# Masking by a minimum on the exponentials, turning left values through DRAM, and an order list for each group

## The chip, the cores and the metric

The kernel runs on one core of one Trainium2 chip. The metric is the device time of one execution, in microseconds; three executions of the kernel before gave 852.54, 853.44 and 858.74, median 853.44.

## The reference, cut to what matters

Two attention layers share one input `x` of 2048 rows by 512 and are mixed row by row with a gate: `g * a + (1 - g) * b`.

```python
# A: 64 segments of 32 rows, 32 heads of 128, 8 memory rows carried along
for s in range(n_seg):
    h = concatenate([mem, x[s]])                  # 8 + 32 rows
    q, k, v = h @ Wq, h @ Wk, h @ Wv              # per head
    scores = where(mask, q @ k.T * scale, -1e9)   # mask: idx_q < 8 or idx_q >= idx_k
    o = (softmax(scores) @ v) @ Wo
    mem = o[:8]; outs.append(o[8:])
# B: 4 blocks of 512 rows, 32 heads of 16, causal softmax attention in the block,
#    plus a linear-attention memory (M, z) of the blocks before, mixed by sigmoid(beta)
```

Segment `s + 1` of A needs the memory rows that segment `s` puts out; B does not depend on A.

## The kernel before, in words

**A.** A group is four consecutive segments. Only 32 of a segment's 40 rows are computed in the chain: 8 memory rows and the first 24 rows of `x`. The last 8 rows of each of the four segments ("left" rows) are projected together, 32 rows at once, ahead of time for the next group (`left_units`): units KL0, KL1, QL0, QL1, VL0, VL1, each a projection of 16 heads on TensorE (L1031 with xL), an evacuation (L387 or L389) and a transpose of 32x32 blocks on VectorE (`flip` L1043, `flip_rows` L1048). Left values are then turned back by matmuls against the identity (units vt0 and vt1, L1090) and evacuated to VL, so that the values of one segment's left rows lie together.

A segment (`segment(s)`) does everything for two halves b of 16 heads, in units that an order list names as `r.unit`, r being the segment in its group:

- `Q0x Q0y K0x ... V1y`: half projections, each two of four 128-row chunks (L1031 with hT); `q0 k0 v0 ...`: evacuations; `TK0 TQ0 ...`: transposes on VectorE; `qt`: GpSimd copies the left queries in.
- `S0 S1`: scores into one PSUM bank, keys as rows. First four matmuls add the mask, `mneg`, by multiplying it with the identity (L1279), then 16 per-head products for the 40 queries (L1282), then 8 products for the left keys (L1287).
- `X0 X1`: exponential on ScalarE into P_sb (L1296). `M0 M1`: sums over keys by matmuls with blocks of ones (L1313). `L0 L1`: logarithm and exponential of the negative on ScalarE, giving 1/sum (L1320, L1323). `N0 N1` on VectorE (L1327) and `n0 n1` on GpSimd (L1333): normalisation.
- `PV0 PV1` and `PL0 PL1`: products with the values (L1343) and the left values (L1355); `E0a ... E1b`: evacuations; `W0a ... W1b`: products with Wo (L1111); `H0 H1`: evacuations; `F0 F1`: folds of four partial sums (L1129); `hm0 hm1`: memory rows into the next segment's hT; `ax0 ax1`: the other rows; `oL`, `xc`: GpSimd copies.
- `ol0 ol1 of`: the output product of a group's left rows, done a group later.

**B** is cut into units that fill A's waits: `bS` (scores, L835), `bE` (exponential of 1024 columns, L854, then a triangle cut on GpSimd), `bP` (values, L887), `bT` (closing work, which has 24 products with the memory, L927). B's own projections come before A, from 5 to 62 us. `tl tb tf` load and write the mixed output of 128 rows.

**Order.** Each engine runs its queue in order. A Python planner walks an order list and appends each unit's operations to the queues of its engines; waits follow from what is read and written. A unit with `e` at the end is the second part of a unit begun before. Units of B and the tail that are not due are skipped, and `relief` runs one when PSUM banks run out. There are three lists: `A_FIRST` for groups 0 to 2, `A_GROUP` for 3 to 14, `A_LAST` for 15. Left units of group 0 run ahead of the lists, one after another:

```python
for u in ("KL0", "KL1", "QL0", "QL1", "VL0", "VL1", "vt0", "vt1"):
    run(first, u)
    run(first, u + "e")
```

DMAs to and from DRAM are issued on SP's queue, in order, each after its waits; A's weights Wk, Wq and Wv are loaded from ScalarE's queue.

Of the kernel before, what the change touches and what calls it, by code (L numbers as in the profile page):

```python
# [5 lines left out]
ALU = mybir.AluOpType  # L6
# [251 lines left out]
def build(nc, es, A_x, A_mem0, A_Wq, A_Wk, A_Wv, A_Wo, B_wq, B_wk, B_wv, B_wo, B_beta, gate_w, out, dbg=None):  # L258
# [31 lines left out]
    def alloc(stack, *specs):  # L290
        at, spans = 0, {}
        for name, shape, dt, n in specs:
# [15 lines left out]
          ("onesb", [128, 128], BF16, 0), ("mneg", [128, 224], BF16, 0),  # L308
# [4 lines left out]
          ("aTg", [128, C, 128], BF16, 0), ("fold", [128, SEG], F32, 0), ("VTL", [128, 4, H // 2, 8, 2], BF16, 0),  # L313
# [3 lines left out]
          ("bmask", [128, 136], BF16, 0), ("mskT", [128, 2, 2, 8, 2], BF16, 0), ("mem0_sb", [128, DM], BF16, 0), ("gwr_sb", [128, 128], BF16, 0), ("beta_sb", [128, HB], BF16, 0),  # L317
# [6 lines left out]
    RT = [128, 4, H // 2, 8, 2]  # L324
    in_a = alloc(esA, ("xL", [128, C, SEG], BF16, 0), ("LN_sb", [128, 2, 512], BF16, 0), ("KTL0", RT, BF16, 0), ("QTL0", LT, BF16, 0), ("VL0", [128, 2, 512], BF16, 0),
          ("KN_sb", [128, 2, 512], BF16, 0), ("QN_sb", [128, 2, 512], BF16, 0), ("KT_sb", LT, BF16, 0), ("QT_sb", [128, H // 2, L, 2], BF16, 0),
          ("V_sb", [128, 2, 512], BF16, 0), ("P_sb", [128, 2, 224], BF16, 0), ("R_sb", [128, 2, 160], F32, 0),
          ("OT_sb", [128, H, L], BF16, 0), ("OTL", [128, H, SEG], BF16, 2), ("KTL1", RT, BF16, 0), ("QTL1", LT, BF16, 0), ("VL1", [128, 2, 512], BF16, 0),
# [13 lines left out]
    dram("aTd", [NG, 128, C, 128])  # L342

# [96 lines left out]
def plan_const(v):  # L440
# [3 lines left out]
    ident, onesb, mneg = v.ident, v.onesb, v.mneg  # L444
    NEG = -1.0e9
# [24 lines left out]
    def late():  # L470
        rob, rmk = Rs("onesb"), Rs("mneg")
        gp(lambda g: g.memset(onesb[:], 0.0), rob, "onesb0", True)
        gp(lambda g: g.memset(mneg[:], 0.0), rmk, "mneg0", True)
        rmt = Rs("mskT")
        gp(lambda g: g.memset(v.mskT[:], NEG), rmt, "mskT0", True)
        for n in range(2):
            gp(lambda g, n=n: g.memset(v.mskT[:, n, n, :, :], 0.0), rmt, "mskT0")
# [4 lines left out]
        for j in range(4):  # L482
            q = slice(32 * j, 32 * j + 32)
            gp(lambda g, q=q: g.memset(onesb[q, q], 1.0), rob, "onesb1_%d" % j)
            for i in range(4):
                o = (L + 16) * i
                sel(mneg[q, o + M:o + L], [[1, 32]], ALU.is_ge, NEG, M, -1, rmk, "mneg1_%d" % j)
            for n in range(2):
                row = v.mskT[q, n, n, :, :]
                for u in range(2):  # L490
                    sel(row[:, :, u], [[-1, 8]], ALU.is_ge, NEG, -16 * u - 8, 1, rmt, "mskT1_%d" % j)
                    sel(row[:, :, u], [[0, 8]], ALU.is_ge, 0.0, -16 * u - 8, 1, rmt, "mskT2_%d" % j)
                    sel(row[:, :, u], [[0, 8]], ALU.is_ge, NEG, -16 if u else 15, 1 if u else -1, rmt, "mskT3_%d" % j)
        v.late_mask = lambda: P.op("dve", lambda d: d.transpose(mneg[:, :].rearrange("p (i w) -> p i w", w=L + 16)[:, :, L:L + 16], v.mskT[:, :, :, :, :].rearrange("p n m k u -> p (n m) (k u)")),
# [276 lines left out]
class BAttn:  # L771
# [178 lines left out]
A_FIRST = """  # L950
    bP bP bT bS 0.Q0x tl bE tl bE 0.Q0y 0.K0x 0.K0y 0.Q1x tb tf 0.q0 bE bT 0.qt 0.Q1y 0.K1x 0.k0 0.K1y 0.TK0 0.q1 bP 0.TQ0 bP 0.TQ1 0.k1 bS 0.V0x 0.S0
    bP bP 0.TK1 0.V0y 0.S1 0.V1x 0.X0 0.V1y 0.M0 QL1 0.X1 0.M1 bE bT 0.v1 0.L0 tbe 0.n0 0.v0 0.N0 tbe VL0 0.xc tf 0.L1 0.PV0 bT tfe 0.PL0 0.n1 KL1 bP
    0.N1 0.E0b 0.E0a 0.PV1 0.PL1 0.W0b 0.E1a 0.E1b 0.W0a 0.W1a tf 0.W1b bP VL1 bT 0.H0 0.F0 tf 0.H1 0.F1 bT tfe 0.hm0 0.hm1 QL0 tl 0.ax0 0.ax1 tf bS
    1.Q0x 1.Q0y 1.K0x 1.Q1x 1.q0 1.K0y bE 1.K1x bE 1.K1y 1.Q1y 1.qt bP 1.k0 1.TQ0 tf 0.oL 1.k1 bE bP 1.TK0 bS tl 1.TK1 bP 1.S0 1.q1 tf 1.V0x 1.TQ1 bS
    1.V1x 1.S1 bP 1.X0 tb 1.M0 bE 1.V0y 1.X1 tfe 1.M1 bT tb tb 1.L0 tfe bE 1.v0 1.V1y tf 1.N0 1.L1 bP tbe bE 1.n0 1.PV0 1.xc bE 1.n1 1.PL0 QL1e 1.E0b
    1.N1 KL0 1.v1 1.E0a 1.PV1 1.PL1 1.W0b 1.E1a 1.E1b 1.W0a bT 1.W1a tbe 1.W1b 1.H0 bS tb bT tfe 1.F0 1.H1 tl 1.oL tl 1.hm0 1.F1 1.hm1 bP 2.qt 2.Q0x
    1.ax0 2.K0x 2.Q0y tbe bT bE bT bS 1.ax1 bE 2.K0y 2.k0 2.Q1x VL1e tfe 2.Q1y bT 2.K1x 2.K1y 2.q0 2.q1 2.TQ0 2.TK0 2.S0 VL0e 2.k1 tl bP tb bP tfe
    2.TQ1 KL1e bS 2.TK1 2.V0x tb 2.X0 bS tl KL0e 2.M0 2.S1 2.V0y 2.V1x ol0 2.L0 2.X1 bP 2.M1 tbe tf 2.n0 2.V1y 2.v0 2.N0 bE 2.PV0 2.PL0 tl 2.L1 2.E0a
    2.v1 2.E0b ol1 bP 2.n1 tb 2.N1 tb 2.PV1 tfe 2.PL1 ol1e 2.W0a 2.E1a 2.E1b 2.W0b 2.W1a 2.W1b vt0 2.H0 bE bS tb tb bT tbe 2.F0 2.H1 2.hm0 2.F1 3.qt
    2.hm1 bP 2.xc 3.K0x vt0e 2.ax0 3.Q0x bP tf bP 3.K0y 3.Q0y bP tfe 3.Q1x 3.K1x 3.Q1y 2.ax1 3.q0 bS 3.k0 bP 3.K1y 3.V0x 3.q1 tl 2.oL 3.TQ0 3.TK0 3.k1  # L960
    tf 3.S0 3.X0 3.TQ1 3.TK1 bE 3.V0y 3.V1x 3.S1 3.M0 3.X1 3.V1y 3.L0 3.v0 tfe of bE 3.M1 3.v1 3.L1 3.n0 3.N0 3.PV0 3.N1 3.n1 3.PL0 3.E0a bE 3.xc bE
    3.PV1 3.PL1 3.W0a 3.E1b QL0e 3.E0b 3.E1a 3.W0b 3.W1b 3.W1a vt1 bS bE bE 3.H0 3.F0 3.H1 tl 3.F1 vt1e bP tbe 3.hm0 3.ax0 3.hm1 bS bT 3.oL tf tf ofe
    3.ax1
    """.split()
A_GROUP = """
# [35 lines left out]
def plan_a(v, nseg):  # L1001
# [48 lines left out]
    def four(t, r, m):  # L1050
        return t[:, r, m, :, :].rearrange("p m k u -> p (m k u)")
# [507 lines left out]
```

## Time and profile before

| | |
|---|---|
| median of three runs | 853.44 us |
| profiled execution | 852.41 us, span 850.6 |
| TensorE matmul | 824.1 us busy (97%), 23047 instructions |
| TensorE weight load | 451.0 (53%) |
| VectorE | 573.9 (67%), 1219 instructions |
| ScalarE | 578.7 (68%), 1412 |
| GpSimd | 252.4 (30%), 619 |
| granted TensorE clock | 1.00 |
| DMA | 51.29 MB, mostly in the first 80 us |

Busy time is the union of an engine's instructions. In a row of a group of instructions, the numbers after the bar are the busy time in us, the mean duration of one in ns, and the idle time of the engine just before them with what ended it. In a timeline row they are start, duration, engine, line, operation, output<-inputs, shape, count.

### The profile page before, as it was taken

To read this page: it belongs to the slowest core of one execution; us is meant where nothing else is said; L and a number is where in the kernel's file an instruction comes from. 1 tells how busy PE (TensorE), PEld (TensorE's weight loads), DVE (VectorE), ACT (ScalarE), POOL (GpSimd) and SP (SyncE) were. 2 spreads that over 40 slices of the span, in tenths; PEclk is the share of its full clock that TensorE was granted. 3 is DMA by queue.
4 is the path that set the end of the run, shared out by engine and by line. 5 is a ranking of instruction groups with operands and counts; after the bars stand their busy time and mean duration, and the time that the engine had idled before them with its cause. 6 is when DMAs were issued, how large, how long until landed. Compare 5 with 4: busy or idle time off the path is not lost.

```text
span 850.6 us, 50542 instructions
## 1 busy us (share of the span) xinstructions
PE 824.1 (97%) x23047; PEld 451.0 (53%) x23054; DVE 573.9 (67%) x1219; ACT 578.7 (68%) x1412; POOL 252.4 (30%) x619
## 2 busy tenths in 40 slices
PE   8998999999999999999999999999999999999997
PEld 4644454555555555555556555555555555555554
DVE  4856566665776767676776767677676767677654
ACT  5765876777677676767676676766767676767554
POOL 3611332323232322333232323233233233223210
PEclk9999999999999999999999999999999999999999
DMA  9997110000011010111111011111111011110011
GB/s 326 407 400 251 22 42 22 16 24 23 23 34 26 20 39 20 33 33 33 30 25 34 21 28 29 33 32 34 30 23 37 20 26 34 32 42 5 16 47 40
DMA packets 63581, 51.29 MB, mean 60 GB/s; under 512 B 33920, under 2 KB 59784, under 8 KB 61832
## 3 DMA queue, kind: packets, MB, share of 16 engines
q1 hardware_dynamic: 61640, 35.48, 14.7%
q10 hardware_dynamic: 1728, 12.58, 3.6%
q8 instruction: 181, 2.97, 1.5%
q14 instruction: 32, 0.26, 0.1%
HBM read 33.47 MB, written 14.57 MB: 56 GB/s over the span
## 4 chain that ended last, share of the span: by engine, by line
PE 89%; DVE 4%; ACT 3%; DMA 2%; issue 1%; DVEq 0%; ACTq 0%
PE ps L1031 48%; PE ps L1111 17%; PE ps L1129 4%; PE ps L1343 3%; PE ps L676 2%; DVE V_sb L389 2%; PE ps L835 2%; PE ps L887 2%; PE ps L1199 1%; PE ps L1282 1%; PE ps L1279 1%; PE ps L1313 1%; DMA scr_kqd<-stgk 1%; DVE P_sb L1327 1%; PE ps L700 1%; DMA Wv_sb<-in_A_Wv_dram 1%
## 5 line engine op out<-in xcount | busy, mean ns | idle before, releaser
L861 POOL TENSOR_SCALAR_AFFINE_SELECT PT<-PT 128x256 bf16<-128x256 bf16 (+2 forms) x160 | 88.5, 553 | 269.8 <-ACT PT L854 264.6
L854 ACT ACTIVATE PT<-ps 128x1024 bf16<-128x1024 f32 x160 | 161.6, 1026 | 5.7 <-PE ps L835 5.5
L1031 PE MATMUL ps<-Wq_sb,hT 128*32 128x512 bf16 x2048 | 144.4, 380 | 0.4 <-ACT hT L387 0.3
L1031 PE MATMUL ps<-Wv_sb,hT 128*32 128x512 bf16 x2048 | 140.7, 379 | 0.7 <-issue 0.4
L1031 PE MATMUL ps<-Wk_sb,hT 128*32 128x512 bf16 x2048 | 139.6, 379 | 0.1
L1111 PE MATMUL ps<-Wo_sb,OT_sb 128*32 128x512 bf16 x2048 | 124.3, 380 | 0.0
L387 ACT ACTIVATE OT_sb<-ps 128x320 bf16<-128x320 f32 x192 | 76.6, 434 | 47.3 <-PE ps L1355 47.0
L389 DVE CAST V_sb<-ps 128x512 bf16<-128x512 f32 x128 | 87.2, 684 | 22.4 <-PE ps L1031 21.8
L387 ACT ACTIVATE KN_sb<-ps 128x512 bf16<-128x512 f32 x128 | 77.1, 602 | 32.9 <-PE ps L1031 31.1
L1333 POOL TENSOR_TENSOR P_sb<-P_sb,R_sb 128x64 bf16<-128x64 bf16 x128 | 48.9, 382 | 145.6 <-ACT R_sb L1323 142.6
L1043 DVE STREAM_TRANSPOSE KT_sb<-KN_sb 128x256 f32<-128x256 f32 x128 | 55.9, 437 | 53.6 <-ACT KN_sb L387 53.3
L387 ACT ACTIVATE WF<-ps 128x256 f32<-128x256 f32 x128 | 42.2, 381 | 73.1 <-PE ps L1111 73.1
L1031 PEld LDWEIGHTS ps<-Wk_sb,hT 128*32 128x32 bf16 x2048 | 55.2, 97 | 49.8 <-ACT PT L854 2.4
L1031 PEld LDWEIGHTS ps<-Wq_sb,hT 128*32 128x32 bf16 x2048 | 53.8, 96 | 50.2 <-ACT hT L387 3.0
L389 DVE CAST QN_sb<-ps 128x512 bf16<-128x512 f32 x64 | 43.8, 684 | 53.5 <-PE ps L1031 53.5
L1043 DVE STREAM_TRANSPOSE QT_sb<-QN_sb 128x256 f32<-128x256 f32 x128 | 56.9, 444 | 25.5 <-ACT QN_sb L387 21.7
L1111 PEld LDWEIGHTS ps<-Wo_sb,OT_sb 128*32 128x32 bf16 x2048 | 48.6, 96 | 44.9 <-ACT OT_sb L387 2.5
L1296 ACT ACTIVATE P_sb<-ps 128x224 bf16<-128x224 f32 x128 | 45.7, 357 | 25.0 <-PE ps L1313 12.6
L389 DVE CAST LN_sb<-ps 128x512 bf16<-128x512 f32 x80 | 54.3, 679 | 10.5 <-PE ps L1031 9.0
L1031 PEld LDWEIGHTS ps<-Wv_sb,hT 128*32 128x32 bf16 x2048 | 46.2, 95 | 26.6 <-ACT KN_sb L387 2.2
L389 DVE CAST OT_sb<-ps 128x320 bf16<-128x320 f32 x64 | 31.3, 489 | 33.1 <-PE ps L1355 33.1
L1320 ACT ACTIVATE R_sb<-ps 128x160 f32<-128x160 f32 x128 | 38.4, 300 | 16.9 <-PE ps L1313 16.1
(132 smaller groups left out, 1433.0 us busy)
## 6 DMA issues: line engine op xcount, KB each, us to landing
Wk_sb<-in_A_Wk_dram ACTq DMA_DIRECT2D x4, 1024.0 KB, 7.8
scr_kqd<-stgk SPq DMA_DIRECT2D x16, 256.0 KB, 7.7
Wq_sb<-in_A_Wq_dram ACTq DMA_DIRECT2D x4, 1024.0 KB, 7.7
Wv_sb<-in_A_Wv_dram ACTq DMA_DIRECT2D x4, 1024.0 KB, 7.7
Wo_sb<-in_A_Wo_dram SPq DMA_DIRECT2D x8, 512.0 KB, 6.8
scr_vd<-V SPq DMA_DIRECT2D x16, 136.0 KB, 6.7
Vj<-scr_vd SPq DMA_DIRECT2D x32, 68.0 KB, 2.5
Wo_sb<-in_A_x_dram SPq DMA_DIRECT2D x8, 256.0 KB, 6.5
```

What stands on the lines that cost most here:

```text
L387: P.op("act", lambda a: a.activation(dst, src, ACT.Copy), reads=[v.rbank[k] for k in bks], writes=dres, name=name)
L389: P.op("dve", lambda d: d.tensor_copy(dst, src), reads=[v.rbank[k] for k in bks], writes=dres, name=name)
L854: P.op("act", lambda a: a.activation(pt[:, :, :], v.ps[:, bks[0]:bks[1] + 1, :], ACT.Exp, scale=v.SCALE_B), reads=[v.rbank[b] for b in bks ...
L861: P.op("gp", lambda g: g.affine_select(mv, mv, [[0, 2], [0, len(cut)], [1, 128]], ALU.is_ge, 0.0, base=0, channel_multiplier=-1), reads=[r ...
L1031: ins = pe.matmul(pb[bk][SEG * j:SEG * (j + 1), :], lhs(c), cols(w, j) if split else w[:, 512 * j:512 * (j + 1)], start=(c == 0), stop=(c ...
L1043: P.op("dve", lambda d: d.transpose(to, src), reads=reads, writes=writes, name=name)
L1111: ins = pe.matmul(pb[bk][SEG * j:SEG * (j + 1), :], lhs(4 * k + j), Wo_sb[:, 4 * k + j, :], start=(first and k == ks[0]), stop=False, skip ...
L1129: ins = pe.matmul(pb[bk][SEG * j:SEG * (j + 1), SEG * n:SEG * (n + 1)], part[:, o:o + SEG], v.fold[:, :], start=True, stop=True, skip_grou ...
L1296: P.op("act", lambda a: a.activation(P_sb[:, b, :], pb[bk][:, 0:224], ACT.Exp, scale=SCALE), reads=[rbank[bk]], writes=[Rs("P%d" % b), Rs( ...
L1320: P.op("act", lambda a: a.activation(R_sb[:, b, :], pb[bk][:, 224:384], ACT.Ln), reads=[rbank[bk]], writes=[Rs("R%d" % b)], name="ln%d_%d" ...
L1333: P.op(ENG["n"], lambda d: d.tensor_tensor(left(P_sb), left(P_sb), grp04(R_sb[:, b, :]), ALU.mult), reads=[Rs("R%d" % b)], writes=[Rs("P%d ...
L1343: ins = pe.matmul(pb[bks[j]][:, L * i:L * (i + 1)], V_sb[SEG * j:SEG * (j + 1), b, i * E:(i + 1) * E], P_sb[SEG * j:SEG * (j + 1), b, LW * ...
```

## The change

The scores are no longer masked in PSUM: the four matmuls per half go, and a new unit `Y0`/`Y1` takes, on VectorE, the minimum of P_sb and `mkeep` (0 where masked, 3e38 elsewhere) between the exponential and the sums. Left rows are ordered row first and segment second. The left values are evacuated as they come into VNL, stored to DRAM when both halves are there, and loaded back by four DMAs into VL, in place of the transposes and of vt0 and vt1; the transposes of the left keys become two each. Each group has a list of its own, which also holds the copy `xl` and, in group 0, that group's own left units (`i` in front). The lists of groups 0 to 14 hold 80 bS, 160 bE and 160 bP among them, the list of group 15 none. The last segment's rows are also marked as written to the tail's input. All lists but part of one are left out here.

```diff
-          ... ("onesb", [128, 128], BF16, 0), ("mneg", [128, 224], BF16, 0),
+          ... ("onesb", [128, 128], BF16, 0), ("mkeep", [128, 224], BF16, 0),
-          ("aTg", [128, C, 128], BF16, 0), ("fold", [128, SEG], F32, 0), ("VTL", [128, 4, H // 2, 8, 2], BF16, 0),
+          ("aTg", [128, C, 128], BF16, 0), ("fold", [128, SEG], F32, 0), ("VNL", [128, 2, 512], BF16, 0),
+    dram("vld", [NG, 128, 2, 4, 128])
-    NEG = -1.0e9
+    KEEP = 3.0e38
-        gp(lambda g: g.memset(mneg[:], 0.0), rmk, "mneg0", True)
+        gp(lambda g: g.memset(mkeep[:], KEEP), rmk, "mkeep0", True)
-                sel(mneg[q, o + M:o + L], [[1, 32]], ALU.is_ge, NEG, M, -1, rmk, "mneg1_%d" % j)
+                sel(mkeep[q, o + M:o + L], [[1, 32]], ALU.is_ge, 0.0, M, -1, rmk, "mkeep1_%d" % j)
...
+A_LIST7 = """
+    0.Q0x 0.Q1x bE 0.Q0y xl 0.K0x 0.qt 0.Q1y 0.q0 0.K0y bE 0.TQ0 0.k0 0.TK0 0.K1x 0.K1y 0.q1 0.V0x 0.xc 0.V0y 0.TQ1 0.k1 0.TK1 0.S0 0.X0 0.V1x 0.S1 tf
+    0.V1y 0.v0 0.Y0 0.M0 0.X1 0.L0 0.n0 bP 0.Y1 tfe bP 0.M1 0.L1 0.N0 0.n1 KL0 0.N1 1.qt 0.PV0 0.PL0 0.E0a 0.E0b 0.v1 KL1 0.PV1 tl 0.PL1 0.E1a 0.W0b 0.E1b
...
     def flip_rows(dst, nat, reads, writes, name):
-        to = dst.rearrange("p r m k u -> p m r (k u)").bitcast(F32)
-        src = nat.bitcast(F32).rearrange("p (m a e) -> p m a e", a=4, e=8)
-        P.op("dve", lambda d: d.transpose(to, src), reads=reads, writes=writes, name=name)
-
-    def four(t, r, m):
-        return t[:, r, m, :, :].rearrange("p m k u -> p (m k u)")
+        src = nat.bitcast(F32).rearrange("p (j m k r) -> p m j k r", m=2, k=8, r=4)
+        for m in range(2):
+            to = dst[:, :, :, :, m, :].bitcast(F32)[:, :, :, :, 0].rearrange("p r j k -> p j k r")
+            P.op("dve", lambda d, to=to, m=m: d.transpose(to, src[:, m, :, :, :]), reads=reads, writes=writes, name=name)
...
-        P.op("gp", lambda gq: gq.tensor_copy(
-            xL[:, :, :].rearrange("p c (r i) -> p c r i", i=8),
-            xT[:, :, 128 * g:128 * (g + 1)].rearrange("p c (r t) -> p c r t", t=SEG)[:, :, :, SEG - 8:SEG]),
-             reads=x_all, writes=[Rs("xL")], name="xl%d" % g)
-        units = {}
+
+        def x_left():
+            P.op("gp", lambda gq: gq.tensor_copy(
+                xL[:, :, :].rearrange("p c (i r) -> p c i r", r=4),
+                xT[:, :, 128 * g:128 * (g + 1)].rearrange("p c (r t) -> p c t r", t=SEG)[:, :, SEG - 8:SEG, :]),
+                 reads=x_all, writes=[Rs("xL")], name="xl%d" % g)
+
+        values = []
+
+        def turn_values():
+            P.dma(P.group("vs%d" % g, "vs"), lambda s: s.dma_start(v.vld[g].rearrange("p b a e -> p b (a e)"), v.VNL[:, :, :]),
+                  reads=[Rs("VNL0"), Rs("VNL1")], writes=[Rs("vld%d" % g)], name="stl%d" % g)
+            grp = P.group("vl%d" % g, "vl")
+            rows = v.vld[g].rearrange("(q r) b a e -> a q (r b) e", r=4)
+            for a in range(4):
+                P.dma(grp, lambda s, a=a: s.dma_start(VL[par][a:128:4, :, :], rows[a]),
+                      reads=[Rs("vld%d" % g)], writes=[Rs("VL%d_%d" % (par, b)) for b in range(2)], name="ldl%d_%d" % (g, a), scratch=True)
+        units = {"xl": x_left}
...
-                    proj(bk, lhs, w_sb, b, True, [Rs("xL"), Rs(wr)], "%sL%d_%d" % (m, g, b))
+                    proj(bk, lhs, w_sb, b, m != "V", [Rs("xL"), Rs(wr)], "%sL%d_%d" % (m, g, b))
                     return lambda: u2(bk, m, b)
 
                 def u2(bk, m, b):
+                    if m == "V":
+                        evac(ENG["VL%d" % b], v.VNL[:, b, :], pb[bk], [bk], [Rs("VNL%d" % b)], "VLev%d_%d" % (g, b))
+                        B.give(bk)
+                        values.append(b)
+                        if len(values) == 2:
+                            turn_values()
+                        return
...
-                    dst, res = (v.VTL, "VTL%d" % b) if m == "V" else (KTL[par] if m == "K" else QTL[par], "%sTL%d_%d" % (m, par, b))
+                    dst, res = KTL[par] if m == "K" else QTL[par], "%sTL%d_%d" % (m, par, b)
...
-                        flip_rows(dst[:, :, 8 * b:8 * (b + 1), :, :], LN_sb[:, b, :], [Rs("LN%d" % b)], [Rs(res)], "%sLt%d_%d" % (m, g, b))
+                        flip_rows(dst[:, :, 4 * b:4 * (b + 1), :, :, :], LN_sb[:, b, :], [Rs("LN%d" % b)], [Rs(res)], "%sLt%d_%d" % (m, g, b))
                 units["%sL%d" % (m, b)] = u
-        for b in range(2):
-            def t(b=b):
...
             def f_sc(pe):
                 ins = None
-                for j in range(4):
-                    rows = slice(SEG * j, SEG * (j + 1))
-                    pe.matmul(pb[bk][rows, 0:224], ident[:, rows], mneg[:, :], start=True, stop=False, skip_group_check=True)
                 for i in range(4):
                     for j in range(4):
                         ins = pe.matmul(pb[bk][SEG * j:SEG * (j + 1), LW * i:LW * i + L], head(KT_sb, 16 * b + 4 * j + i),
-                                        head(QT_sb, 16 * b + 4 * j + i), start=False, stop=True, skip_group_check=True)
+                                        head(QT_sb, 16 * b + 4 * j + i), start=True, stop=True, skip_group_check=True)
                 for k in range(2):
                     for j in range(4):
                         m = 8 * b + 2 * j
-                        ins = pe.matmul(heads4(pb[bk][SEG * j:SEG * (j + 1), 0:4 * LW])[:, 2 * k:2 * k + 2, L:LW], four(KTL[par], r, slice(m, m + 2)),
+                        ins = pe.matmul(heads4(pb[bk][SEG * j:SEG * (j + 1), 0:4 * LW])[:, 2 * k:2 * k + 2, L:LW], KTL[par][:, r, m // 2, :, :, :].rearrange("p k m u -> p (k m u)"),
                                         QT_sb[:, m + k, :, :].rearrange("p (a q) u -> p u a q", q=8)[:, :, 0::4, :],
-                                        start=False, stop=True, skip_group_check=True)
+                                        start=True, stop=True, skip_group_check=True)
                 return ins
-            P.op("pe", f_sc, reads=[Rs("KT%d" % b), Rs("QT%d" % b), Rs("QTl"), Rs("KTL%d_%d" % (par, b)), Rs("mneg"), Rs("ident")],
+            P.op("pe", f_sc, reads=[Rs("KT%d" % b), Rs("QT%d" % b), Rs("QTl"), Rs("KTL%d_%d" % (par, b))],
                  writes=[rbank[bk]], name="sc%d_%d" % (s, b))
 
         def expo(b):
             bk = sbk[b]
             P.op("act", lambda a: a.activation(P_sb[:, b, :], pb[bk][:, 0:224], ACT.Exp, scale=SCALE),
                  reads=[rbank[bk]], writes=[Rs("P%d" % b), Rs("P%dL" % b)], name="exp%d_%d" % (s, b))
+
+        def mask(b):
+            P.op(ENG["y"], lambda d: d.tensor_tensor(P_sb[:, b, :], P_sb[:, b, :], mkeep[:, :], ALU.min),
+                 reads=[Rs("mkeep")], writes=[Rs("P%d" % b), Rs("P%dL" % b)], name="msk%d_%d" % (s, b))
...
-                    ins = pe.matmul(grp04(pb[bks[j]][:, 0:4 * L]), VL[par][SEG * j:SEG * (j + 1), b, 128 * r:128 * (r + 1)],
+                    ins = pe.matmul(grp04(pb[bks[j]][:, 0:4 * L]), VL[par][SEG * j:SEG * (j + 1), 2 * r + b, :],
...
-            P.op("gp", lambda gq: gq.tensor_copy(QT_sb[:, :, SEG:L, :], QTL[par][:, :, 8 * r:8 * r + 8, :]),
+            P.op("gp", lambda gq: gq.tensor_copy(QT_sb[:, :, SEG:L, :], QTL[par][:, :, r:SEG:4, :]),
...
-    for u in ("KL0", "KL1", "QL0", "QL1", "VL0", "VL1", "vt0", "vt1"):
-        run(first, u)
-        run(first, u + "e")
-    rest = {}
+    rest = {"i" + u: fn for u, fn in first.items()}
...
-        for u in ORDERS[2 if ending else g > 2]:
+        for u in ORDERS[g]:
```

## The prediction

> **What bounds the kernel now.** I read the page's busy times first, then the groups of instructions by shape, then TensorE's timeline for one segment, then the chain in order of time.
>
> ```profile
> span 850.6 us, 50542 instructions
> PE 824.1 (97%) x23047; PEld 451.0 (53%) x23054; DVE 573.9 (67%) x1219; ACT 578.7 (68%) x1412; POOL 252.4 (30%) x619
> PEclk9999999999999999999999999999999999999999
> ```
>
> TensorE looks full at a full clock, VectorE and ScalarE are two thirds full. The timeline shows what TensorE's 97% is made of (start, duration, instruction):
>
> ```profile
> 405.37 0.60 PE L1031 MATMUL ps<-Wv_sb,hT 128*32 128x512 bf16 x8
> 405.81 0.27 PE L1279 MATMUL ps<-mneg,ident 128*32 128x224 bf16 x4
> 405.90 0.27 PE L1282 MATMUL ps<-QT_sb,KT_sb 128*32 128x40 bf16 x16
> 406.00 0.21 PE L1287 MATMUL ps<-QT_sb,KTL 128*32 128x32 bf16 x8
> 406.06 1.03 PE L1031 MATMUL ps<-Wv_sb,hT 128*32 128x512 bf16 x16
> 406.92 0.27 PE L1313 MATMUL ps<-P_sb,onesb 128*32 128x160 bf16 x8
> 409.00 0.41 PE L1090 MATMUL ps<-ident,VTL 128*32 128x128 bf16 x16
> 409.24 1.03 PE L1199 MATMUL ps<-woB_sb,oTg 128*32 128x512 bf16 x16
> ```
>
> A matmul's duration includes a pipeline that the next one overlaps, so what an item costs is the distance from its start to the next start: a half projection 0.43, the four mask products 0.09 to 0.10, the scores without them 0.155, the sums 0.095, a turn of left values (L1090) 0.22 to 0.24. Read so for every unit from the first left projection (about 60.8) to 847, the items make 722 us of 786: 64 us are waits, most of them hidden inside "busy". The chain shows the rhythm, one group of four segments being the distance between two equal rows:
>
> ```profile
> 305.88 4.00 PE ps L1031 x72
> 353.83 4.00 PE ps L1031 x72
> 401.98 4.00 PE ps L1031 x72
> ```
>
> That is 48.1 us a group, with items for 45.2: waits 2.9. The first three groups take about 50.6 with items for 44.8: waits 5.8. So TensorE's own work bounds the kernel, and the chain from one segment's memory to the next one's is close behind it.
>
> **The parts of the change, costed.** These rows carry the prices:
>
> ```profile
> L1279 PE MATMUL ps<-mneg,ident 128*32 128x224 bf16 x512 | 35.0, 260 | 0.0
> L1090 PE MATMUL ps<-ident,VTL 128*32 128x128 bf16 x512 | 12.8, 220 | 1.1 <-DVE VTL L1048 1.1
> L1327 DVE TENSOR_TENSOR P_sb<-P_sb,R_sb 128x160 bf16<-128x160 bf16 x128 | 42.2, 331 | 5.8 <-ACT R_sb L1323 5.5
> L664 DVE TENSOR_SCALAR etmp<-etmp 128x512 bf16<-128x512 bf16 x24 | 7.1, 294 | 2.2 <-ACT etmp L659 2.1
> L389 DVE CAST VL<-ps 128x512 bf16<-128x512 f32 x32 | 21.9, 688 | 6.1 <-PE ps L1090 5.9
> L1048 DVE STREAM_TRANSPOSE VTL<-LN_sb 128x256 f32<-128x256 f32 x32 | 14.2, 445 | 1.1
> ```
>
> *TensorE.* The mask products go: 128 half segments by 0.095 = 12.2 us. The turns go: 32 by 0.22 = 7.0 us. Together **-19.2 us**. Both stand behind their waits, in the order of the queue, so they are not hidden by anything. The Trainium skill ("Perfetto Trace Analysis", Identifying the Most-Contended Engine) says that matmul busy time misjudges pipelined work; the trace agrees, since the busy column would promise 35.0 + 12.8 = 47.8 us for the same two groups, and with that the kernel would come to about 808.
>
> *VectorE.* Added: 128 minima of 128x224. Nothing in the trace is a two-source bf16 operation throughout. Low end: L664 does 512 elements of one source in 294 ns, so 0.22 to 0.29. High end: L1327 scaled, 331 + 64 elements at 0.96 a ns = 0.40. I take 0.33, between, as L1327 is the nearest by operation but has an f32 source. The Trainium skill ("VectorE: DVE Perf Modes", the perf-mode tier table) has a bf16 tensor_tensor at two elements a cycle, which I estimate at 0.27; no row here shows it. Gone: 32 casts by 688 = 21.9 and 32 transposes by 445 = 14.2. The 32 KTL transposes become 64 of half the size; from 445 less 128 elements at one per 1.04 ns, 0.31 each, +5.7. Net 42 - 36 + 6 = +12 us over 790, from 67% to about 70%: not a bound by itself.
>
> *The wait.* The minimum comes between the exponential and the sums. The smallest distance that the trace has from the start of the mask products to the sums is 0.93, so 0.68 from the end of the scores; now 0.68 plus the minimum plus a hand-over of about 0.05, or 1.0 to 1.13. Behind the waiting minimum in VectorE's queue stand V casts, transposes and normalisations; behind the waiting sums stand the next projections. What covers it is what the list puts between S and M: before, 0.90 in the median; in the new lists 1.19, with 0.96 for a quarter of the halves. The cover was lengthened by about the price. If it were not there, 128 by 0.35 = 45 us would show.
>
> *The lists.* The three old lists name B units that are often not due; the new ones name exactly the 80 score, 160 exponential and 160 value units that there are, all in the first fifteen groups, as now (the last B product in the profile is at 785.9). So no item is added or lost by them.
>
> *Left values through DRAM.* Per group one store of 256 KB and four loads of 64 KB on SP's queue, 80 issues in all. Nearest rows: 256 KB landed in 7.7 us while the weights loaded, 64 KB (pQj) in 2.5, and one issue took 0.3 to 0.6. The loads wait for the store, so SP is held for 4 to 8 us a group, and behind it stand the K, Q and V loads of B, the tail's loads and the output stores. SP idles most of the span, and from VL1's evacuation to the next group's PL0 the lists leave some 24 us: nothing, after group 0. In group 0 the store stands behind the Wo loads, issued until 72.7, with the DMA engines busy until about 79; then four issues and 2.5 us land the values at about 84. PL0 is due 14.7 us of items after 60.8, near 79 with waits: **+5 us**.
>
> *The start.* The first left units now stand between projections. Now they take 8.7 us (60.8 to 69.5) for 5.6 of items: **-3 us**; the late Wv (a wait of 1.4) is covered by two half projections and B scores.
>
> *GpSimd* keeps its copies, the mask constants their number: 0.
>
> **The sum.** -19.2 + 5 - 3 = -17, if the waits stay what they are: 2.9 a group in the steady part. The profiled execution took 852.4 (span 850.6 and 1.8 around it), 1.0 under the median of the runs; so 835.4 in its terms, 836.4 against the median, rounded to **837**.
>
> **The rivals.**
> *The chain takes over (within 1%).* I went down both orders of TensorE with the smallest distances that the trace shows (S to M above; sums to PV 1.5; V pass to PV 1.0; last Wo product to the two folds 0.65 and 0.95; fold to the next projection 0.5), adding each shortfall once. Before: 1.6 of the 2.9 us in a steady group, 35 in all. After: 2.8 a steady group, 57 in all, of which some 2 go for the 24 B memory products that I left out. That is +20 and gives 837 + 20 = 857, or about 850 if lists made per group lose less behind busy ScalarE and VectorE than the remaining 29 us of today. For it: less TensorE work is left to fill the same chain. Against: the smallest distances are not the ones that an order sees, and the first three groups show that waits follow the list (5.8 against 2.9 with almost equal items).
> *Slower: the minimum stands behind casts.* In VectorE's order by the new lists, 38 of 128 minima come right after a V or left-value cast of 0.68 and 50 after a transpose of 0.44. If each is late by half of that, 38 by 0.34 + 50 by 0.22 = 24 us, on top of the +20 with half of it overlapping: 837 + 32 = 869. It decides once the sums start more than some 1.2 us after the scores end, the median cover. For it: VectorE is in order and 70% full. Against: the cast is placed there because the exponential is still running.
> *Better lists.* If the waits fall by a third everywhere, 64 to 43: 837 - 21 = 816. For it: 29 us are waits that no dependence explains. Against: less work to fill with.
> *No saving at all* would need mask products that ran in a wait; the timeline has them behind their wait, without a gap.
>
> **How the numbers follow.** Forecast (waits stay) 0.42, better lists 0.10, chain takes over 0.30, minimum behind casts 0.18. The measurement tells about 1% (8.5 us) from no change. Faster by more than that: the first two less a little of the forecast's edge, plus the chain's lower edge: 0.52. Same: 0.27. Slower: 0.21. The range reaches from the better lists' near half, 818, to 864, between the two slower cases; the likeliest case alone, with the minimum at 0.22 or 0.40 and the group 0 wait at 0 or 8, has 828 to 845.
>
> **What would show it.** Right: no mask and turn products, some 22,000 matmul records; 47.0 us a steady group with items for 44.0; minima near 0.3; PL0 of group 0 waiting about 5 us for a DMA and no DMA wait later; VectorE near 70%. Wrong: a steady group at 48 with waits before the sums or PV (chain), minima whose releaser is a cast (second rival), B's K, Q or V loads late behind the left values' loads, or a clock under full after group 0's wait.

## The result, and the profile after

The kernel after takes 860.34 us (median of 12 runs, 857.55 to 865.50) against 853.36 for the kernel before on the same chip: a ratio of 1.0075, with a 95% interval of 1.0049 to 1.0100. The prediction had 837 and faster; it came out slower by three quarters of a per cent, inside the range of 818 to 864 but on the other side of no change.

The page of the kernel after, first the span and busy times, then the granted clock in 40 slices:

```profile
span 859.2 us, 48664 instructions
PE 816.6 (95%) x22030; PEld 425.3 (49%) x22030; DVE 572.9 (67%) x1315; ACT 582.7 (68%) x1412; POOL 255.7 (30%) x619
PEclk9999899999999999999999999999999999999999
```

TensorE is less busy, by 1,017 matmuls, in a longer span, and one slice is under the full clock. The added operation costs what it should; groups by shape on VectorE, with busy time and mean ns after the bar:

```profile
L1453 DVE TENSOR_TENSOR P_sb<-P_sb,mkeep 128x224 bf16<-128x224 bf16 x128 | 36.2, 285 | 11.3 <-ACT P_sb L1449 9.6
L1205 DVE STREAM_TRANSPOSE KTL<-LN_sb 128x128 f32<-128x128 f32 x64 | 26.2, 409 | 2.2
L390 DVE CAST VNL<-ps 128x512 bf16<-128x512 f32 x32 | 21.9, 687 | 14.4 <-PE ps L1187 8.5 <-DMA scr_vld<-VNL 5.7
```

The third row holds a first clue: VectorE stood 5.7 us before a cast, for the store of the left values.

I measured groups from the first sums of one to the first sums of the next, in TensorE's timeline. Counted by their columns, at the rate of the half projections (0.43 us for 2 x 512), TensorE's items from the first sums to the last product shrank from 687.4 to 667.2 us, by 20.2 where 19.2 was forecast; what lies between them grew from 82.8 to 110.4.

| us | first sums at | group 0 | 1 | 2 | mean of 3 to 13 | 14 | 15, to the end |
|---|---|---|---|---|---|---|---|
| before | 76.8 | 50.0 | 51.1 | 49.2 | 48.15 | 47.1 | 46.8 |
| after | 78.1 | 60.1 | 49.8 | 48.2 | 48.23 | 46.2 | 46.4 |

So there are two losses: 10 us in group 0, and a steady group in which 1.2 us less work takes as long as before. Group 0 first, all engines' timeline (SPq is a DMA issue):

```profile
75.98 1.26 SPq L1222 DMA_DIRECT2D scr_vld<-VNL  x1
78.39 1.13 PE L1187 MATMUL ps<-Wq_sb,xL 128*32 128x512 bf16 x16
83.33 2.50 SPq L1227 DMA_DIRECT2D VL<-scr_vld  x4
83.33 0.69 DVE L390 CAST VNL<-ps 128x512 bf16<-128x512 f32 x1 [5.66 <-DMA scr_vld<-VNL]
84.54 0.55 DVE L1484 TENSOR_TENSOR P_sb<-P_sb,R_sb 128x160 bf16<-128x160 bf16 x2
85.00 0.32 PE L1500 MATMUL ps<-P_sb,V_sb 32*128 32x40 bf16 x16 [5.48 <-DVE P_sb L1484]
88.72 0.24 PE L1512 MATMUL ps<-P_sb,VL 32*128 32x64 bf16 x4 [3.40 <-DMA VL<-scr_vld]
88.89 1.90 PE L1187 MATMUL ps<-Wq_sb,xL 128*32 128x512 bf16 x16
```

The store is issued at 75.98, behind the Wo loads, and has landed at 83.33. VL0e of the *next* group writes the same VNL, so its cast waits for that store, and the normalisations stand behind the cast in VectorE's queue: TensorE waits 5.48. Only then do the four loads come, and TensorE waits another 3.40. The last row is a projection at half speed (1.90). Before, the same products followed one another without a wait, and a left projection took 1.05:

```profile
79.02 0.27 PE L1343 MATMUL ps<-P_sb,V_sb 32*128 32x40 bf16 x16
79.13 0.20 PE L1355 MATMUL ps<-P_sb,VL 32*128 32x64 bf16 x4
79.26 1.05 PE L1031 MATMUL ps<-Wk_sb,xL 128*32 128x512 bf16 x16
```

The stretch after by windows: TensorE's busy time, then the granted clock, the DMA share and GB/s:

```profile
80.00:82.00 2.00, 0.00 (x0) 1.00 0.56 204
82.00:84.00 2.00, 0.00 (x0) 0.70 0.05 20
90.00:92.00 2.00, 2.00 (x40) 0.50 0.00 0
92.00:94.00 2.00, 2.00 (x36) 0.74 0.04 8
```

For the steady groups the timeline shows one place well: segment 1, from the products with left values (PL0) to the next half's products with values (PV1). Before:

```profile
433.11 0.20 PE L1355 MATMUL ps<-P_sb,VL 32*128 32x64 bf16 x4
433.23 0.30 PE L887 MATMUL ps<-PT,Vj 128*32 128x128 bf16 x8
433.36 0.40 PE L1090 MATMUL ps<-ident,VTL 128*32 128x128 bf16 x16
433.96 0.28 PE L1343 MATMUL ps<-P_sb,V_sb 32*128 32x40 bf16 x16 [0.21 <-DVE V_sb L389]
```

And after:

```profile
441.62 0.21 PE L1512 MATMUL ps<-P_sb,VL 32*128 32x64 bf16 x4
441.76 0.30 PE L888 MATMUL ps<-PT,Vj 128*32 128x128 bf16 x8
442.47 0.28 PE L1500 MATMUL ps<-P_sb,V_sb 32*128 32x40 bf16 x16 [0.41 <-ACT OT_sb L388]
```

0.85 us with a turn of left values in it, 0.85 without: that turn seems to have run in a wait, which an experiment below tests.

### The profile page after: what moved, and what is told of

Read it like the earlier page. It is cut to its first block, busy times and chain, and to the rows that moved or that the text cites. A ratio compares the mean times of both kernels' runs of the same rounds, so it can differ in the third digit from the quotient of the medians.

```text
span 859.2 us, 48664 instructions
## 1 busy us (share of the span) xinstructions
PE 816.6 (95%) x22030; PEld 425.3 (49%) x22030; DVE 572.9 (67%) x1315; ACT 582.7 (68%) x1412; POOL 255.7 (30%) x619
## 4 chain that ended last, share of the span: by engine, by line
PE 86%; ACT 5%; DMA 4%; DVE 3%; issue 1%; POOL 0%; SPq 0%; DVEq 0%; POOLq 0%; ACTq 0%
PE ps L1187 45%; PE ps L1266 17%; PE ps L1284 4%; PE ps L1500 3%; PE ps L677 3%; PE ps L836 3%; PE ps L888 2%; PE ps L1470 2%; PE ps L1355 2%; PE ps L1435 2%; PE ps L701 1%; DVE V_sb L390 1%; DMA Wv_sb<-in_A_Wv_dram 1%; DMA scr_kqd<-stgk 1%; ACT PT L855 1%
## 5 line engine op out<-in xcount | busy, mean ns | idle before, releaser
L855 ACT ACTIVATE PT<-ps 128x1024 bf16<-128x1024 f32 x160 | 159.4, 1026 | 1.3 <-PE ps L836 0.6
L1187 PE MATMUL ps<-Wq_sb,hT 128*32 128x512 bf16 x2048 | 136.2, 380 | 0.6 <-ACT hT L388 0.3
L1187 PE MATMUL ps<-Wv_sb,hT 128*32 128x512 bf16 x2048 | 136.6, 379 | 0.0
L1187 PE MATMUL ps<-Wk_sb,hT 128*32 128x512 bf16 x2048 | 134.5, 379 | 0.9 <-ACT hT L388 0.2
L1266 PE MATMUL ps<-Wo_sb,OT_sb 128*32 128x512 bf16 x2048 | 128.5, 382 | 1.1 <-ACT OT_sb L388 1.1
L1187 PEld LDWEIGHTS ps<-Wk_sb,hT 128*32 128x32 bf16 x2048 | 53.4, 96 | 51.5 <-ACT hT L388 2.6
L1500 PEld LDWEIGHTS ps<-P_sb,V_sb 32*128 32x128 bf16 x2048 | 23.4, 92 | 64.4 <-DVE P_sb L1484 24.9
L1500 PE MATMUL ps<-P_sb,V_sb 32*128 32x40 bf16 x2048 | 35.3, 178 | 18.0 <-DVE P_sb L1484 7.6
```

The lines of the kernel that those rows point to most:

```text
L855: P.op("act", lambda a: a.activation(pt[:, :, :], v.ps[:, bks[0]:bks[1] + 1, :], ACT.Exp, scale=v.SCALE_B), reads=[v.rbank[b] for b in bks ...
L1187: ins = pe.matmul(pb[bk][SEG * j:SEG * (j + 1), :], lhs(c), cols(w, j) if split else w[:, 512 * j:512 * (j + 1)], start=(c == 0), stop=(c ...
L1266: ins = pe.matmul(pb[bk][SEG * j:SEG * (j + 1), :], lhs(4 * k + j), Wo_sb[:, 4 * k + j, :], start=(first and k == ks[0]), stop=False, skip ...
L1500: ins = pe.matmul(pb[bks[j]][:, L * i:L * (i + 1)], V_sb[SEG * j:SEG * (j + 1), b, i * E:(i + 1) * E], P_sb[SEG * j:SEG * (j + 1), b, LW * ...
```

## The experiments

Ratios are to the kernel before, with 95% intervals; "x 853.4" turns one into us. Steady groups are means of groups 3 to 13 of one profile. Line numbers differ from kernel to kernel.

**Group 0.** Wo loads 4 to 7 go behind the left values' store and loads; everything below called "Wo later" has this edit.

```diff
-        if 58 < n < 63:
+        if 58 < n < 61:
...
                             turn_values()
+                            if g == 0:
+                                for q in range(4, 8):
+                                    v.wo_load(q)
```

> The changed kernel with the second half of Wo (four loads of 512 KB) issued on SP's queue after group 0's left values have been stored and loaded back, instead of before. Theory 'late store': group 0 took 60.1 us against 50.0 because the store of its left values stood behind Wo; the waits of 5.5 (VectorE held by the next group's value cast) and 3.4 (PL0 by the DMA) shrink to at most 3 together, group 0 comes to 52 to 54, the kernel to 852 to 855. Rival 'group 0's list': the order itself holds the wait, group 0 stays near 60 and the kernel at 860.

858.99, ratio 1.0041 (1.0005 to 1.0077): between the two theories. The wait behind VectorE's cast falls from 5.48 to 0.69; the products with left values still wait 3.60. Group 0 takes 57.2, the steady groups 48.18 as before. Next, the same without any store or load (the left values are cast straight into VL):

> The changed kernel with the later Wo loads, and the turn through DRAM left out: the left values are cast straight to where the turned ones should lie, so there is no store and there are no loads (the products with the left values then use unturned rows). If the turn holds the steady groups back (SP's queue, the loads, the DMA engines): 840 to 848, 47.2 a steady group or less. If it costs only in group 0, where the products with left values waited 3.6 us for the load: 859 less 3 to 5, so 854 to 856, with steady groups at 48.2 as they are. If even that wait only moves on: 858.

853.21, 0.9965 (0.9935 to 0.9996). Group 0 takes 50.3, as before the change, and the steady groups 48.18, as the second branch had it: the way through DRAM costs some 6.5 us, in group 0, and in these lists nothing later. Two attempts to shorten it:

```diff
-    for res, dst, src in (("Wk", ...), ("Wq", ...), ("Wv", ...)):
+    for res, dst, src in (("Wk", ...), ("Wv", ...), ("Wq", ...)):
# and iQL0, iQL1 exchanged with iVL0, iVL1 in group 0's list
```

> The changed kernel with the later Wo loads, Wv loaded ahead of Wq, and group 0's own left values projected ahead of its left queries, so that their way through DRAM starts some 2.5 us earlier. If that way is what group 0 waits for: the wait of the first products with left values falls from 3.6 to about 1, and the time from 859 to 856. If the left queries, now last, hold the first scores back by as much: 859 with the first sums later. If group 0's loss without a turn (6 us) is not the way's length: no change in that wait.

860.68, 1.0076 (1.0044 to 1.0107), the wait still 3.52. But the way did not start 2.5 us earlier: the store went out 9.0 us after the first left projection, against 9.6 in the kernel with Wo later, and took 7.7 us to land (75.69 to 83.42), over 1 us longer; two pairs of Wo loads were ahead of it. So this run does not tell what an earlier start is worth, and the last one puts the store ahead of all Wo loads:

> The changed kernel with all Wo loads behind the store of group 0's left values: the store first, then two of the eight Wo loads, the four loads of turned values, and the other six. In the kernels with the Wo loads moved, the store still took 6.6 and 7.7 us to land, behind Wo loads that were under way, where it takes 2.8 later on. If that is the length of the way: the store lands in about 3 us, the first products with left values wait under 1 us instead of 3.6, and the time falls from 859 to 855, a ratio of 1.000 to 1.002. If the products with Wo then wait as much longer: 858 to 860.

859.62, 1.0050 (1.0022 to 1.0078). The wait fell as its first branch said, the time went as its second; TensorE's waits of this kernel (total, times, longest):

```profile
PE ps L1505 <- ACT OT_sb L388: 6.8, 14, 0.7
PE ps L1271 <- DMA Wo_sb<-in_A_Wo_dram: 2.9, 2, 1.7
```

The store's way now takes 2.2 us and the products with left values wait 0.93, but Wo is late, and the clock is at half from 84.2 to 94.5. The DMA engines are full up to 88 (columns as above, the share and GB/s last):

```profile
82.00:84.00 2.00, 1.43 (x40) 1.00 1.08 367
84.00:86.00 2.00, 0.76 (x8) 0.56 1.10 351
86.00:88.00 2.00, 1.13 (x12) 0.50 1.10 348
```

The 4 MB of Wo and the left values share one stretch: of the orders tried, each made one of them late.

**What the removed products were worth.** The kernel before without any mask (mask products left out, nothing in their place):

> The kernel before with the mask products left out and nothing in their place: no mask is applied at all. Everything else as before. If the chain holds the end in the old order too: 850 to 854, the 0.76 us a group of products turning into waits. If TensorE's work bounds the old order: 853.4 - 12.2 = 841, a steady group of 47.4. The new order without any mask came to the time that it has with the minimum; the question here is whether the old one does the same.

846.58, 0.9910 (0.9877 to 0.9942): 7.7 of 12.2 us, between the branches. Most steady groups take 47.4; in their mean, 0.76 us of items are gone and waits are 0.28 longer (0.16 before the V projections, 0.14 before B's scores). Now the turns, 15 of 16 products of each left out:

```diff
-                    for q in range(4):
-                        for j in range(4):
+                    for q in range(1):
+                        for j in range(1):
```

> The kernel before with each turn of left values cut to one of its 16 products (15 of 16 left out; the transposes ahead of it, the bank and the evacuation stay). If the turns stood behind their waits, as the prediction had it: 32 x 0.21 = 6.6 us less, a ratio of 0.992, a steady group of 47.75. If both turns of a group ran in waits between the products with left values and the next half's products with values (PL0 to PV1 takes 0.84 to 0.85 us in segment 1 with a turn in it before, and without one after): no change, a ratio of 1.000, PL0 to PV1 in segment 1 still at 0.85. If only segment 1's did: 3.3 us less, 0.996.

852.71, 0.9987 (0.9963 to 1.0012): 1.1 of 6.6 us, between the last two branches, with an interval that includes no change. The same place in segment 1:

```profile
436.81 0.19 PE L1355 MATMUL ps<-P_sb,VL 32*128 32x64 bf16 x4
437.06 0.22 PE L1090 MATMUL ps<-ident,VTL 128*32 128x128 bf16 x1
437.66 0.28 PE L1343 MATMUL ps<-P_sb,V_sb 32*128 32x40 bf16 x16 [0.39 <-DVE V_sb L389]
```

0.85 again: what the turn no longer fills becomes a wait (0.21 to 0.39). In segment 3 the distance fell from 1.33 to 1.15, so the other turn did count. Both cuts together:

> The kernel before with no mask at all and the turns cut to one of 16 products: what the removed products are worth together in the old order, with nothing put in their place. If all of them count: 853.4 - 12.2 - 6.6 = 834.6, a ratio of 0.978. If they count as the masks alone did (8.5 of 12.2) and the turns as one of two: 841 to 843, a ratio of 0.986. If the chain is next after the masks: 846, as without masks alone.

844.97, 0.9892 (0.9866 to 0.9918): 9.2 us of the 18.8 that were left out, where the prediction had all of its 19.2.

**What the minimum costs.** The kernel before with the minimum alone, right behind each exponential, in the old lists:

> The kernel before with one part of the change: the mask products go and the minimum is taken on VectorE right behind each exponential; old lists, left values turned on TensorE. If the chain from one segment's memory to the next holds the end in every order (waits fill what the mask products leave): 851 to 857, a steady group of about 48.1 with waits of 3.7 where it had 2.9. If the old lists could use the products' 0.76 us a group and only the new lists or the turn through DRAM give it away: 841 plus what the minimum's own wait costs, so 841 to 850. If the minimum is what costs: above 860, and well above the same kernel without any mask.

891.71, 1.0438 (1.0391 to 1.0484): 45 us above the same kernel without a mask: the last branch, far above its 860. TensorE's waits (total, times, longest), sums for the minimum on top:

```profile
PE ps L1313 <- DVE P_sb L1296: 17.1, 36, 0.8
PE ps L1343 <- DVE P_sb L1327: 8.9, 8, 1.8
```

Groups 0 to 2 take 55.1, 57.8 and 53.9, a steady one 49.39. In groups 0 to 2 of this profile the clock was at half for 13.7 us, and TensorE worked for 12.3 of them, so by my estimate up to 6 us of their loss are the clock's; in the steady groups it was full. Two ways to find room for it in the old lists: the minimum where the list names the sums, and each sums unit behind TensorE's next unit.

> The kernel before with the minimum on VectorE, taken where the list names the sums instead of right behind the exponential: VectorE first does the casts and transposes that the list has between the two. If it was the minimum's waiting for the exponential that held VectorE's queue up: below 891.7 by 10 or more. If the minimum comes later for it and the sums wait longer: 895 to 915, with over 2.05 us a group before the sums. If neither: 885 to 895.

886.48, 1.0334 (1.0280 to 1.0388): the last branch, with the longer wait of the second. Of the 9.0 us between the two profiles 5.1 are in groups 0 to 2 (54.2, 55.5, 51.9), with 6.8 us at half clock instead of 13.7, and 4.9 ahead of the first sums, which vary from profile to profile; a steady group takes 49.60, with 2.31 before the sums. Where the minimum stands in VectorE's queue is a fifth of its 45 us at most.

> The kernel before with the minimum on VectorE behind each exponential, and in its three lists each sums unit moved behind the next unit of TensorE (a half projection, scores, the other sums), with what hangs on it. If the minimum only needs its cover and the old lists have it to give: the wait before the sums, 2.05 us a steady group in the kernel with the minimum alone, falls to about 0.3, nothing else grows, a group takes 47.6 to 47.8 and the whole 847 to 856. If the cover is one stock that the sums and the products with the values share: the wait moves to PV (1.23 a group there) and a group stays at 48.2 to 49.4, the whole at 858 to 890.

895.90, 1.0466 (1.0432 to 1.0499); steady groups 49.76, slower than either branch. The wait before the sums falls from 1.99 (2.05 by the expectation's count) to 1.08, but PV gains 0.61 and the left projections 0.46: one stock of cover, as the second branch said, though it put the time too low. Now the new lists, without and with a second minimum (both Wo later):

> As e1_wo_later, with the minimum left out: no mask is applied at all, neither by TensorE nor by VectorE. Theory 'the minimum's wait eats the saving': the sums start 0.3 us earlier after the scores, steady groups fall by 0.8 to 1.2 to about 47, total 12 to 18 us under e1_wo_later. Rival 'the shortfalls lie elsewhere': the time saved before the sums is lost before the values and folds, steady groups fall by 0.1 to 0.3, total 1 to 4 us under e1_wo_later.

860.83, 1.0053 (1.0017 to 1.0088): with the minimum 1.0041. In the new order leaving the minimum out gains nothing that shows in the time, to some 4 us; a steady group falls by 0.11, as the rival said.

> The changed kernel with the later Wo loads and every minimum taken twice in a row (the second changes nothing), so 0.28 us more between exponential and sums, 128 times. If the new lists' cover is sized to one minimum: most of 128 x 0.28 = 36 us shows, 880 to 895. If there is slack beyond it: 859 to 866. Leaving the only minimum out had moved the time by under 2 us.

878.71, 1.0266 (1.0234 to 1.0298): 19 of 36 us show, a little under the first branch, and the wait before the sums rises from 0.31 to 1.76. The new lists cover one minimum and about half of a second.

> The changed kernel with the later Wo loads, and the normalisation left out on VectorE and GpSimd: the products with the values then wait for the minimum and their own operands, not for sums, logarithm, exponential and multiplication. If the waits before PV (1.88 us a steady group, the largest) come from that chain: a group falls from 48.2 to 47.2 or less, the whole to 840 to 846. If they come from the evacuations that free PV's banks (ScalarE and VectorE): 855 to 859, with 1.6 or more left before PV.

852.77, 0.9963 (0.9937 to 0.9990): between the branches. A steady group falls by 0.4, to 47.77, but 1.66 of the 1.82 before PV stay. The largest releaser there is ScalarE's evacuation of the half before: 9.3 us in 17 waits now, and 6.8 in 14 with the normalisation, which released 2.6 in 6.

The steady group, in us; the rows below the first are the time before an item beyond what the item before it needs for its columns, at the rate of the half projections (0.43 for 2 x 512):

| | before | old lists, no mask, turns cut | old lists, minimum | the same, late sums | new lists, no mask | new lists, minimum | minimum twice |
|---|---|---|---|---|---|---|---|
| group | 48.15 | 47.44 | 49.39 | 49.76 | 48.07 | 48.18 | 49.37 |
| sums (M) | 0.18 | 0.15 | 1.99 | 1.08 | 0.11 | 0.31 | 1.76 |
| PV | 1.25 | 1.50 | 1.23 | 1.84 | 1.93 | 1.82 | 1.73 |
| K, Q projections | 0.09 | 0.07 | 0.06 | 0.08 | 0.43 | 0.46 | 0.43 |
| all | 4.35 | 4.79 | 6.34 | 6.71 | 5.42 | 5.53 | 6.72 |

The second and the fifth column have the same items on TensorE (42.65 us). They differ by the lists and what comes with them (the way through DRAM, the order of the left rows, the two-part key transposes): 0.63 us a group. The minimum adds 0.11.

**Orders and masks crossed.** New lists and the turn through DRAM, but the mask as products on TensorE (Wo later):

> As e1_wo_later, with the mask added by TensorE as before the change and no minimum; lists and DRAM turn are the new ones. Theory 'the minimum's wait eats the saving': steady groups pay 0.76 us for the mask products and get back the wait for the minimum, so 47.9 to 48.3 a group as in e1_wo_later, total within 3 us of it. Rival 'the lists' shortfalls lie elsewhere' (sums to values, Wo to folds): the products come on top, 48.8 to 49.2 a group, total 8 to 12 us over e1_wo_later.

868.47, 1.0134 (1.0055 to 1.0214), as the rival said; steady 48.85, 0.67 above the minimum's 48.18. Exchanging products for the minimum is worth 8 us in the new order (to some 7, as the intervals are wide), much as leaving the mask out is in the old one. The old lists with the turn through DRAM and mask products (this kernel also has the change's order of left rows and two-part key transposes):

> The three lists of before and the mask on TensorE; of the change only the left values' turn through DRAM is kept (no turn products, no left-value transposes), with Wo's second half after group 0's values. Theory 'items count where the list has cover': 32 turns by 0.22 go, waits rise by about 0.4 a group, total 847 to 851 if group 0 costs no more than 2 us over before. Rival 'the chain is full already': waits rise by as much as the items fall, 0.44 a group, and the total is 852 to 856.

877.79, 1.0247 (1.0180 to 1.0315); a steady group 49.26, 1.1 above before with less work, and groups 0 and 1 take 61.4 and 53.7. Neither branch held. The waits lie before many items (PV 1.60, the products with Wo 0.80, B's scores 0.55), but most of them end with VectorE: between 230 and 760 us TensorE waits 14.0 us in 42 waits for its casts and transposes, against 2.3 in 11 before, which is the 1.1 a group. What makes VectorE late there I did not find. The kernel before with the new lists alone, each turn ahead of an H0:

> The kernel before with the new lists alone: mask products on TensorE, the left values turned on TensorE (each turn put right ahead of the products' evacuation of the segment after its projection's), group 0's own left units ahead of everything as before. If the new lists are what holds the steady groups back: 860 to 868, a steady group of 48.9 to 49.3. If the turn through DRAM is: 850 to 856, a steady group of 48.1 or less. If neither alone is, and the chain is: 853 to 858 with waits of 2.9 to 3.3 a group.

890.01, 1.0422 (1.0368 to 1.0476). The place that I gave the turns costs at least 9 of these 36 us by itself: the folds wait for a bank that a left-value cast on VectorE empties (9.2 us in 10 waits). So this run doesn't price the lists; with the one before, it suggests that a list fits the units that it was made for.

**A mixture.** The minimum only in the 36 halves where the old lists cover it, in place of their products:

```diff
+        late = lambda b: 3 <= g <= 14 and (r, b) in ((1, 0), (2, 0), (2, 1))
...
+            if late(b):
+                P.op("dve", lambda d: d.scalar_tensor_tensor(P_sb[:, b, :], mneg[:, :], 998244352.0, P_sb[:, b, :], ALU.add, ALU.min), ...)
```

> The kernel before, with the mask on VectorE only where the old lists cover it: in groups 3 to 14 for both halves of segment 2 and the first of segment 1, whose sums waited 0.03 us or less with the minimum in every half (the others waited 0.14 to 0.72). There the mask products go and VectorE takes the minimum of the exponentials and mneg + 998244352, which is 0 where masked; every other half keeps its products. If covered minima are free: 36 x 0.095 = 3.4 us less, 2.4 by what masks were worth in the old order, a steady group of 47.9, a ratio of 0.996 to 0.997. If VectorE's longer queue costs elsewhere: a ratio of 1.000 or more and a steady group of 48.15 or more.

856.82, 1.0011 (0.9989 to 1.0033), a steady group 48.16. TensorE has 0.29 us less in a group and waits 0.28 more in sum (PV 0.20, the V projections 0.15), though the sums wait only 0.06 more: the second branch. VectorE spends 357 ns on this form, and delays behind it are the likely reason; which of them count was not tried. So no version that computes the whole reference beat the kernel before.

## Why the prediction was wrong, step by step

**"-19.2 ... not hidden by anything" is the first step that failed.** The count of TensorE's work was right (20.2 us less from the first sums on); its worth was 9.2. Standing behind a wait in the queue doesn't mean that an item delays what follows: what follows the turn of segment 1 waits for an evacuation that ends at the same moment anyway. The timeline of before had this: a 0.21 wait right behind the turn. Of the masks, 7.7 of 12.2 us counted, and part of the rest came back as waits before the V projections and B's scores.

**"If the waits stay what they are" is the second.** The prediction said that the cover was lengthened by about the price, and that holds: the minimum's wait is gone (0.31 a group before the sums). It counted the cover itself at nothing. PV waits 0.57 us more a group than before, and the K and Q projections 0.37. With the items of mask and turn gone in both orders, the new lists and what comes with them take 0.63 a group more than the old ones, and the minimum another 0.11. I put that down to the V projections, left projections and B pieces that now stand between scores and sums and are missing elsewhere; moving the sums in the old lists showed such a shift, but no run took the pieces back one by one. In ratios x 853.4: products gone, 844.2; new order with the minimum, no turn, 850.4; with the way through DRAM, 856.9; with the Wo loads ahead, 859.8; each to some 2 to 3, so that the +6.2 of the second step is known to some 3.5.

That "45 us would show" without the cover agrees with the old lists (891.7 against 846.6) partly by luck: it was 0.35 for each half, and came as 1.7 a steady group, which is 0.21 a half, and 18 us in groups 0 to 2, where part was the slower clock.

**The group 0 term, +5, measured +9.4** (6.5 for the way and 2.9 for the Wo loads by the ratios, 6.9 and 2.9 in the profiles' groups 0). The way through DRAM behind the Wo loads was seen, and its 3.4 at PL0; missed were the cast of the next group behind the store, with the normalisations behind it, and the slower clock, which the prediction had only among its signs. As TensorE worked for 4.6 us at half clock there, I estimate that the clock makes 2.3 of it. "Nothing, after group 0" held in the new lists.

**Smaller terms.** The minimum took 0.28 where I took 0.33; the Trainium skill's rate ("VectorE: DVE Perf Modes", the perf-mode tier table), estimated there at 0.27, agrees. The trace did have an operation with two bf16 sources: L665, 692 ns for 512 elements; it is another operation (SCALAR_TENSOR_TENSOR), and such a form took 0.357 in the mixture. The half-size transposes took 0.41, not 0.31: half the elements, nine tenths of the time. The start was misread: the first left projection begins at 59.7 and ends at 60.8, so the units that I put at 8.7 us took 9.8. The -3 came in part: from there to the first sums it takes 15.8 us after and 17.1 before, with Wv waiting 1.37 as it did. The first sums are 1.3 later all the same, because B's own projections, ahead of the change, ended 2.6 later in that profile; over all profiles the first left projection begins between 59.7 and 69.6. The sum's 836.4 was rounded up to 837, which matters to nothing here.

**The rivals.** "The chain takes over" came near: it has 857, and with group 0 larger by 4.4 than its +5, 861. Part of that is luck, since the start went otherwise than it had it and groups 1, 2, 14 and 15 took 3.6 less. Its tally of smallest distances gave the 1.2 us a group that were lost, but its cause (less work to fill the same chain) covers only 0.44 of them, what waits grew by in the old lists when the products went; the other 0.74 came with the new order and its minimum at the same items, most of it before PV and the K and Q projections. "Minima behind casts" did not come: TensorE's waits for minima in the kernel after come to 0.7 us.

## What to carry to other kernels

Before counting a removed item as saved time, look at what starts next and what released it: an item whose follower waits anyway is free already. Treat work that covers a wait as a stock: a new link in a chain is paid from it even when its own wait disappears from the profile, so look for waits elsewhere. And when a buffer is written back by a DMA, look for its next writer: that one carries the DMA's delay into a queue that had nothing to do with it.

## What the runs showed of the hardware

A wait of TensorE can cost twice. In the kernel after, its last product before the pause ended near 79.5; the granted clock was 1.00 until 82, 0.70 from 82 to 84, 0.50 until 92 and 0.74 in the two us after, though TensorE worked again from 88.7. So it fell some 3.3 us into the pause and came back some 4 us after it; meanwhile a left projection took 1.90 instead of 1.05. In the profile of the kernel without a turn no such pause occurs and the clock stays at 1.00. The Trainium skill says so ("TensorE: Matmul & The Clock Gate", What's actually happening): half rate after an idle window of about 3.4 us, full rate after as long a busy one. This trace agrees.

But a long pause is not needed. In the kernel with the store first, the clock fell at 84.2, 0.6 us after a product, with no pause of over 1 us in the 3.4 us before; TensorE had been busy for 1.7 of them. In the old lists with the minimum it fell four times in groups 0 to 2, each time after 3.4 us with 1.5 to 1.7 of work. The stretches at half clock lasted 3.4, 6.8 or 10.2 us in every profile here, but for the one at a kernel's end.
